# A Fourier layer and a gated feed-forward layer on one core: the end of batch 0's last inverse step moved into the first two token tiles, and the bias sum shared between GpSimd and TensorE

## The chip, the cores and the metric

One core of a Trainium2 chip. The metric is the device time of one execution in microseconds (us). Each kernel was timed in several executions. The profile is of one execution.

## The reference

```python
# attention part: b = 8 batches, 3008 positions, 256 channels
X = np.fft.rfft(x, axis=1)
Yr = Xr @ w_r - Xi @ w_i + b_r
Yi = Xr @ w_i + Xi @ w_r + b_i
# soft threshold of Yr and Yi at 0.01, then
y = np.fft.irfft(Y, n=3008, axis=1)
# feed-forward part on 24064 tokens, d_ff = 2048
h = y @ w_in
r = np.maximum(h, 0.0)
g = s * (r * r) + b
out = g @ w_out
```

The constant b contributes b times the column sums of w_out to each row of the output. The kernel computes that once, as `bias_bc`.

## The kernel before

The transform of 3008 = 94 x 32 points is done by matmuls. Batch 0 is transformed alone at the start (some 47 us). After that TensorE works through token tiles, and the transforms of the later batches are interleaved with the tiles in small units. Batch 0 ends with a transpose back (`turn`) and the last DFT (`last_dft`), for two halves ec of the 256 channels and for 32 values of n2. The first three token tiles read only n2 below 16.

```python
# end of first_batch(), ec = 1 (the second half of the channels e)
for k in range(4):
    turn(1, k)            # two PSUM banks: 4 transposes and a copy of 512 columns each
    some(1)               # a matmul of batch 1's first step (u)
    if k:
        last_dft(1, 8 * (k - 1))   # two banks: 4 DFTs and a copy of 384 columns each
last_dft(1, 24)
...
def evac(dst, src, cols, scale=None):    # a copy out of PSUM, to the less loaded engine
    ta, td = 0.17 + cols / 1200.0, 0.15 + cols / 960.0
    if load["act"] + ta <= load["dve"] + td:
        load["act"] += ta
        ...                               # ScalarE
    load["dve"] += td
    ...                                   # VectorE
...
def sum_w_out():          # GpSimd: all 16 row groups of w_out, in fp32
    for q in range(4, MC, 2):
        nc.gpsimd.tensor_tensor(out=acc, in0=acc, in1=w_out_t[:, q : q + 2], op=ALU.add)
    nc.gpsimd.tensor_tensor(out=w_sum, in0=acc[:, 0], in1=acc[:, 1], op=ALU.add)
def make_bias():          # one matmul with ones adds the 128 partitions
    nc.tensor.matmul(ps[:, 0:D], ones, w_sum, start=True, stop=True)
...
# in a token tile, for each pair of 128 columns of d_ff:
nc.scalar.activation(out=rt, in_=ps, func=AF.Relu)                   # ScalarE
nc.vector.tensor_tensor(out=gt, in0=rt, in1=rt, op=ALU.mult)         # the square, VectorE (or ScalarE, by load)
...
load.update(act=0.0, dve=0.0)    # between first_batch() and the tiles
```

The PSUM pool of the tiles (`psh`, two buffers of two banks) takes the place of the first batch's pool (`psm`, four banks). `psf` and `psa` have two banks each.

Of the kernel before, what the change touches and what calls it, by code (L numbers as in the profile page):

```python
# [9 lines left out]
F16 = mybir.dt.float16  # L10
F32 = mybir.dt.float32
ALU = mybir.AluOpType
AF = mybir.ActivationFunctionType

P = 128
N1 = 94
N2 = 32
# [79 lines left out]
def kernel(  # L97
# [13 lines left out]
    nc = tc.nc  # L111
    B, S, D = x.shape
# [4 lines left out]
    MC = DFF // P  # L117
    H = NPAIR // 2
    HW = N2 // 2
# [24 lines left out]
    cpool = ctx.enter_context(tc.tile_pool(name="consts", bufs=1))  # L144
# [20 lines left out]
    def evac(dst, src, cols, scale=None):  # L165
# [3 lines that stand above are left out]
            if scale is None:  # L169
                return None, nc.scalar.copy(out=dst, in_=src)  # L170
            return None, nc.scalar.mul(out=dst, in_=src, mul=scale)
        load["dve"] += td
        if scale is None:
            return nc.vector.tensor_copy(out=dst, in_=src), None
        return nc.vector.tensor_scalar_mul(out=dst, in0=src, scalar1=scale), None
# [3 lines left out]
    def mix_bank():  # L179
        return pools["m"].tile([P, 512], F32, name="psm", tag="psm")  # L180
# [3 lines left out]
    def any_bank():  # L184

        turn_of[0] += 1
        if "h" in pools:
            return (other_bank, one_bank)[turn_of[0] % 2]()
        return (mix_bank, one_bank, mix_bank, other_bank)[turn_of[0] % 4]()
# [4 lines left out]
    def one_bank():  # L194
        return fpool.tile([P, 512], F32, name="psf", tag="psf")

    def other_bank():
        return apool.tile([P, 512], F32, name="psa", tag="psa")
# [20 lines left out]
    ones = cpool.tile([P, P], F16, name="ones")  # L219
# [33 lines left out]
    eye_t = cpool.tile([P, P], F16, name="eye_t")  # L253
# [7 lines left out]
    bb_bc = cpool.tile([P, 1], F32, name="bb_bc")  # L261
# [22 lines left out]

    w_in_t = [cpool.tile([P, DFF], F16, name=f"w_in_{dc}") for dc in range(DC)]
    w_out_t = cpool.tile([P, MC, D], F16, name="w_out_t")
    bias_bc = cpool.tile([P, 2, D], F32, name="bias_bc")

    def emit_load_weights():
        for dc in range(DC):  # L290
            nc.gpsimd.dma_start(out=w_in_t[dc], in_=moe_w_in[dc * P : (dc + 1) * P, :])
        nc.gpsimd.dma_start(
            out=w_out_t, in_=moe_w_out.rearrange("(mc p) d -> p mc d", p=P)
        )


    neg_lam = cpool.tile([P, 1], F32, name="neg_lam")
# [35 lines left out]
            )  # L333
            nc.vector.tensor_copy(out=blocks(F_2[0])[r, :, 1, a], in_=F_c[r, :, 0])

    w_sum = cpool.tile([P, D], F16, name="w_sum")

    def sum_w_out():
        acc = opool.tile([P, 2, D], F32, name="acc", tag="ost")
        nc.gpsimd.tensor_tensor(  # L340
            out=acc, in0=w_out_t[:, 0:2], in1=w_out_t[:, 2:4], op=ALU.add
        )
        for q in range(4, MC, 2):
            nc.gpsimd.tensor_tensor(out=acc, in0=acc, in1=w_out_t[:, q : q + 2], op=ALU.add)
        nc.gpsimd.tensor_tensor(out=w_sum, in0=acc[:, 0], in1=acc[:, 1], op=ALU.add)

    def make_bias():
        ps = other_bank()
        nc.tensor.matmul(ps[:, 0:D], ones, w_sum, start=True, stop=True)
        for j in range(2):  # L350
            nc.scalar.activation(
                out=bias_bc[:, j], in_=ps[:, 0:D], func=AF.Copy, scale=bb_bc
            )

    us = {}
    vs = {}
# [6 lines left out]
    def first_batch():  # L363
# [3 lines left out]
        for g in range(N2 // 4):  # L367
            c, h = divmod(g, 2)
            for dc in range(DC):
                ps = one_bank() if dc else mix_bank()  # L370
                with tc.issue_after(last_pe.ins):
                    for j in range(4):
# [4 lines left out]
                            start=True, stop=True,  # L377
# [35 lines left out]
        vt = bigpool.tile([P, DC, N2, 96], F16, name="vt", tag="corr")  # L413
# [69 lines left out]
        for h in range(2):  # L483
            vs[(0, h)] = vspool.tile([96, HW, D], F16, name="vs", tag="vs")

        def turn(ec, k):
            for i in range(2):
                ps = any_bank() if ec else mix_bank()
                n = 8 * k + 4 * i
                for j in range(4):  # L490
                    nc.tensor.matmul(
                        ps[0:96, j * P : j * P + P], vt[:, ec, n + j, :], eye_t,
                        start=True, stop=True,
                    )
                h, n = divmod(n, HW)
                evac(
                    vs[(0, h)][:, n : n + 4, ec * P : (ec + 1) * P],
                    ps[0:96].rearrange("p (j e) -> p j e", e=P), 512,
                )

        yt = yts[0] = ypool.tile([P, DC, N2, 96], F16, name="yt", tag="yt")

        def last_dft(ec, n2):

            if ec or n2 >= 16:
                ps = [any_bank(), any_bank()]
            else:
                ps = [one_bank(), other_bank()]
            for j in range(8):
                h, k = divmod(n2 + j, HW)  # L510
                nc.tensor.matmul(
                    ps[j // 4][:, (j % 4) * 96 : (j % 4) * 96 + 96],
                    vs[(0, h)][:, k, ec * P : (ec + 1) * P], C_t,
                    start=True, stop=True,
                )
            for i in range(2):
                evac(
                    yt[:, ec, n2 + 4 * i : n2 + 4 * i + 4, :],
                    ps[i][:, 0:384].rearrange("p (j n) -> p j n", n=96), 384,
                )  # L520

        more = s1_units(1, True)

        def some(n):
            for _ in range(n):
                if more:
                    more.pop(0)()

        steps = [(ec, u) for ec in range(DC) for u in range(U)]
        for i in range(2 * U + 2):  # L530
            if i < 2 * U:
                mix(*steps[i])
            if 0 <= i - 1 < 2 * U:
                fwd_dft(*steps[i - 1])
            if 0 <= i - 2 < 2 * U:
                inv_dft(*steps[i - 2])
            k = i - U - 2
            if 0 <= k < 4:
                turn(0, k)
            for n in {1: (0,), 2: (8,), 4: (16, 24)}.get(k, ()):  # L540
                last_dft(0, n)
            if i >= 2 * U:
                some(3)
            if i == 9:

                gate = nc.gpsimd.tensor_copy(out=low[0:1, 0, 0:1], in_=vt[0:1, 1, 0, 0:1])
                with tc.issue_after(gate.ins):
                    make_w_g()
                    make_bounds()
                    sum_w_out()  # L550
        for k in range(4):
            turn(1, k)
            some(1)
            if k:
                last_dft(1, 8 * (k - 1))
        last_dft(1, 24)
        return more


    def s1_units(b, more_banks=False):  # L560
# [264 lines left out]
    def second_mms(ti):  # L825

        tl = tiles[ti]
        w = width(tl)
        size = sub_size(tl)
        nsub = -(-w // size)  # L830
        hold = {}

        def mm(sub, mc):

            alone = ti == len(tiles) - 1 and sub >= 2
            h = 0 if alone else sub % 2
            if h == 0 and mc == 0:
                hold["ps"] = other_bank().rearrange("p (h e) -> p h e", h=2)
            ps = hold["ps"]
            nc.tensor.matmul(  # L840
                ps[0:size, h, :], gts[(ti, mc // 2)][:, mc % 2, sub * size : (sub + 1) * size],
                w_out_t[:, mc, :],
                start=(mc == 0), stop=(mc == MC - 1),
            )
            if sub == nsub - 1 and mc % 2 == 1:
                gts.pop((ti, mc // 2))
            if mc == MC - 1 and (alone or h == 1 or sub == nsub - 1):
                k = h + 1
                ost = opool.tile([P, 2, D], F32, name="ost", tag="ost")
                nc.vector.scalar_tensor_tensor(  # L850
                    out=ost[0:size, 0:k], in0=ps[0:size, 0:k], scalar=s_bc[0:size],
                    in1=bias_bc[0:size, 0:k], op0=ALU.mult, op1=ALU.add,
                )
                load["dve"] += 0.12 + 0.27 * k
                for i in range(k):
                    store(tl, sub - k + 1 + i, ost[:, i, :])

        return [lambda s=s, m=m: mm(s, m) for s in range(nsub) for m in range(MC)]


    plan = {}

    def schedule(start, span, units):
        for i, u in enumerate(units):
            plan.setdefault(start + (i * span) // len(units), []).append(u)

    with tc.tile_pool(name="psm", bufs=4, space=bass.MemoryType.PSUM) as pool:
        pools["m"] = pool
        more = first_batch()
    pools["h"] = ctx.enter_context(  # L870
        tc.tile_pool(name="psh", bufs=2, space=bass.MemoryType.PSUM)
    )
# [6 lines left out]
        if tl[0] == "main" and tl[2] == 0 or tl[0] == "wide" and tl[2] == (0, 0):  # L879
            mark[tl[1]] = i * MC  # L880
    schedule(0, 10, more)
    plan.setdefault(15, []).append(make_bias)
    plan.setdefault(17, []).append(load_x_2)
    schedule(24, 42, s23_units(1))
    schedule(mark[1] - 12, 16, s4_units(1))
    for b in range(2, B):
# [51 lines left out]
```

## Time and profile before

| | us |
|---|---|
| time, median of the first 3 runs | 847.02 (846.86 to 847.43) |
| span of the profiled execution | 845.0 |
| first w_in matmul (first token tile) | 47.90 |
| GpSimd ends the sum of w_out | 50.00 |
| first matmul of batch 1's forward transform | 62.91 |

The page's first part gives each engine's busy time; the chain that ended last is followed back from the end, so an engine's share of it is time that counted. The timeline lists start, length, engine, line, operation and tiles, and in square brackets how long the engine had been idle and what ended that. Three lines of before's timeline are needed later, GpSimd's last add, VectorE's first four squares and the first forward matmul of batch 1 (columns as said):

```profile
49.28 0.72 POOL L345 TENSOR_TENSOR w_sum<-acc 128x256 f16<-128x256 f32 x1
...
50.15 4.67 DVE L783 TENSOR_TENSOR gt<-rt 128x1024 f16<-128x1024 f32 x4 [1.18 <-ACT rt L776]
...
62.91 0.61 PE L606 MATMUL psf<-F_t,us 128*128 128x128 f16 x8
```

GpSimd ends at 50.00, 0.15 us before the first square starts. Four squares take 4.67 us, 1.15 us from start to start.

### The profile page before, as it was taken

Reading aid. Unit: us, or ns where it says so; the run is one execution under the profiler, and the core shown is the slowest. Engines: PE = TensorE matmul, PEld = TensorE weight load, DVE = VectorE, ACT = ScalarE, POOL = GpSimd, SP = SyncE. Lnnn points to the kernel's source line nnn. Section 1 sums busy time; section 2 is a strip of 40 time slices with the busy share of each in tenths; the row PEclk is TensorE's granted clock in tenths of the full one; section 3 lists DMA queues with packets and bytes.
Section 4 is the critical chain, followed back from the end, with each engine's and each line's share of the span. In section 5 each row is a group of like instructions: output and inputs, shape, how many; then the busy total and the mean of one; then the engine's idle time right before and its main releaser. Section 6 shows DMA issues by size and latency. Waiting matters only on the chain.

```text
span 845.0 us, 17114 instructions
## 1 busy us (share of the span) xinstructions
PE 833.8 (99%) x6653; PEld 599.6 (71%) x6653; DVE 693.6 (82%) x1026; ACT 641.8 (76%) x864; POOL 45.0 (5%) x71
## 2 busy tenths in 40 slices
PE   8999999999999999999999999999999999999997
PEld 6857767777677766777677776777667777766765
DVE  5989987888888987888888888798978888776674
ACT  5988887778778877787777787778877878766673
POOL 5331000000000001000000000000000000000000
PEclk9999999999999999999999999999999999999999
DMA  8945567124752367324761248513354223411111
GB/s 202 180 143 122 121 173 203 57 77 101 203 154 56 101 169 190 92 68 107 189 175 49 81 103 205 160 42 91 113 144 125 64 74 95 112 33 38 38 44 50
DMA packets 105746, 96.06 MB, mean 114 GB/s; under 512 B 9542, under 2 KB 97482, under 8 KB 104322
## 3 DMA queue, kind: packets, MB, share of 16 engines
q1 hardware_dynamic: 99218, 80.55, 33.0%
q0 software_dynamic: 6448, 14.42, 10.6%
q8 instruction: 52, 0.85, 0.4%
q14 instruction: 28, 0.23, 0.1%
HBM read 53.52 MB, written 46.66 MB: 119 GB/s over the span
## 4 chain that ended last, share of the span: by engine, by line
PE 90%; ACT 3%; DMA 3%; DVE 2%; issue 1%; POOL 0%; SPq 0%; ACTq 0%; DVEq 0%; POOLq 0%
PE psa L840 37%; PE psh L769 36%; PE psf L635 4%; PE psf L570 2%; PE psf L621 2%; PE psf L606 2%; PE psf L665 2%; PE psf L718 2%; ACT rt L776 2%; PE psm L426 1%; DMA x<-in_x_dram 1%; DMA ud<-u 1%; DVE gt L783 1%; DMA us<-ud 1%; DMA F_c<-dft_fwd 0%
## 5 line engine op out<-in xcount | busy, mean ns | idle before, releaser
L776 ACT ACTIVATE rt<-psh 128x1024 f32<-128x1024 f32 (+2 forms) x384 | 386.7, 1008 | 119.6 <-PE psh L769 117.5
L783 DVE TENSOR_TENSOR gt<-rt 128x1024 f16<-128x1024 f32 (+2 forms) x322 | 385.7, 1202 | 95.4 <-ACT rt L776 94.5
L840 PE MATMUL psa<-w_out_t,gt 128*128 128x256 f16 (+1 forms) x3024 | 454.4, 272 | 0.1
L840 PEld LDWEIGHTS <-gt 128*128 128x128 f16 (+1 forms) x3024 | 300.9, 101 | 187.0 <-issue 1.4
L769 PE MATMUL psh<-yt,w_in 128*128 128x512 f16 (+1 forms) x1344 | 396.3, 378 | 0.2 <-ACT rt L776 0.2
L769 PEld LDWEIGHTS <-w_in 128*128 128x128 f16 x1536 | 142.8, 98 | 27.3 <-issue 1.8
L850 DVE SCALAR_TENSOR_TENSOR ost<-psa,s_bc,bias_bc 128x512 f32<-128x512 f32 (+2 forms) x97 | 71.1, 733 | 10.0 <-PE psa L840 8.2
L780 ACT ACTIVATE gt<-rt 128x1024 f16<-128x1024 f32 (+2 forms) x62 | 65.3, 1054 | 1.0
L640 DVE TENSOR_TENSOR ring<-psf,s 128x512 f16<-128x512 f32 x84 | 57.5, 685 | 3.8 <-PE psf L635 3.3
L170 ACT CAST v<-psf 128x512 f16<-128x512 f32 x78 | 45.3, 583 | 19.7 <-PE psf L665 19.7
L170 ACT CAST xf<-psf 128x512 f16<-128x512 f32 x82 | 47.9, 586 | 10.9 <-PE psf L606 10.9
L170 ACT CAST u<-psf 96x512 f16<-96x512 f32 x76 | 43.9, 580 | 12.4 <-PE psf L570 12.2
L769 PE MATMUL psh<-tail,w_in 128*128 128x512 f16 (+1 forms) x192 | 52.1, 353 | 0.0
L635 PE MATMUL psf<-W_g,xf 128*128 128x256 f16 x336 | 50.4, 273 | 0.0
L170 ACT CAST yt<-psf 128x480 f16<-128x480 f32 (+2 forms) x73 | 37.8, 525 | 11.6 <-PE psf L718 11.6
L213 POOL DMA_DIRECT2D x<-in_x_dram x36 | 18.7, 526 | 430.3 <-PE psf L570 429.2
L570 PE MATMUL psf<-x,A_t 94*96 94x512 f16 x103 | 39.3, 382 | 1.1 <-ACT yt L170 0.5
L646 DVE TENSOR_TENSOR ring<-ring,high 128x512 f16<-128x512 f16 x84 | 35.6, 423 | 2.3
L647 DVE TENSOR_TENSOR ring<-ring 128x512 f16<-128x512 f16 x84 | 35.5, 423 | 2.0
L645 DVE TENSOR_TENSOR ring<-ring,low 128x512 f16<-128x512 f16 x84 | 35.4, 421 | 1.6
L635 PEld LDWEIGHTS <-xf 128*128 128x128 f16 x336 | 32.9, 98 | 3.8
L718 PE MATMUL psf<-C_t,vs 96*128 96x96 f16 x448 | 33.2, 205 | 0.2 <-ACT yt L170 0.2
(97 smaller groups left out, 499.5 us busy)
## 6 DMA issues: line engine op xcount, KB each, us to landing
out_dram<-ost SPq DMA_DIRECT2D x152, 128.0 KB
ud<-u SPq DMA_DIRECT2D x28, 384.0 KB
us<-ud SPq DMA_DIRECT2D x28, 384.0 KB
vd<-v SPq DMA_DIRECT2D x42, 256.0 KB
vs<-vd SPq DMA_DIRECT2D x14, 768.0 KB
x<-in_x_dram POOLq DMA_DIRECT2D x28, 376.0 KB, 5.9
ring<-ring SPq DMA_DIRECT2D x280, 32.0 KB
out_dram<-ost SPq DMA_DIRECT2D x16, 120.0 KB
```

Source lines behind the costliest of these rows:

```text
L170: return None, nc.scalar.copy(out=dst, in_=src)
L570: nc.tensor.matmul(ps[0:96, :], A_t[0:N1, :], x16[(b, c)][0:N1, j * D : (j + 2) * D], start=True, stop=True,)
L635: nc.tensor.matmul(ps[:, r, :], xt[:, 2 - r, dc], W_g[:, dc, r], start=(dc == 0), stop=(dc == DC - 1),)
L640: nc.vector.tensor_tensor(out=t, in0=ps, in1=hold[i // 2][:, i % 2].unsqueeze(1).to_broadcast([P, 2, D]), op=ALU.add,)
L646: nc.vector.tensor_tensor(out=m, in0=m, in1=high, op=ALU.min)
L718: nc.tensor.matmul(ps[:, j * 96 : (j + 1) * 96], vs[(b, h)][:, k, ec * P : (ec + 1) * P], C_t, start=True, stop=True,)
L769: nc.tensor.matmul(o, w_in_t[dc][:, mc * P : (mc + 1) * P], r, start=(dc == 0), stop=(dc == DC - 1),)
L776: nc.scalar.activation(out=rt[:, :, 0:w], in_=ps[:, :, 0:w], func=AF.Relu)
L780: nc.scalar.activation(out=gt[:, :, 0:w], in_=rt[:, :, 0:w], func=AF.Square)
L783: nc.vector.tensor_tensor(out=gt[:, :, 0:w], in0=rt[:, :, 0:w], in1=rt[:, :, 0:w], op=ALU.mult)
L840: nc.tensor.matmul(ps[0:size, h, :], gts[(ti, mc // 2)][:, mc % 2, sub * size : (sub + 1) * size], w_out_t[:, mc, :], start=(mc == 0), sto ...
L850: nc.vector.scalar_tensor_tensor(out=ost[0:size, 0:k], in0=ps[0:size, 0:k], scalar=s_bc[0:size], in1=bias_bc[0:size, 0:k], op0=ALU.mult, o ...
```

## The change

Its intent: the first token tiles need only half of n2, so the other half of ec = 1 need not hold them up. Its transposes and last DFTs go into slots 10 to 24 of the tiles (a slot is one group of 128 columns of d_ff). The tiles then start earlier, and the bias must be ready earlier; so GpSimd adds 12 of the 16 row groups of w_out and TensorE accumulates the other four and the two halves of GpSimd's sum in PSUM.

```diff
-        nc.gpsimd.dma_start(
-            out=w_out_t, in_=moe_w_out.rearrange("(mc p) d -> p mc d", p=P)
-        )
+        for q in (slice(0, 12), slice(12, MC)):
+            nc.gpsimd.dma_start(out=w_out_t[:, q], in_=...[:, q])
 ...
-        for q in range(4, MC, 2):
+        for q in (4, 6, 8):
             nc.gpsimd.tensor_tensor(out=acc, in0=acc, in1=w_out_t[:, q : q + 2], op=ALU.add)
-        nc.gpsimd.tensor_tensor(out=w_sum, in0=acc[:, 0], in1=acc[:, 1], op=ALU.add)
+        nc.gpsimd.tensor_tensor(out=w_sum, in0=acc, in1=w_out_t[:, 10:12], op=ALU.add)
 ...
-        nc.tensor.matmul(ps[:, 0:D], ones, w_sum, start=True, stop=True)
+        parts = [w_out_t[:, q] for q in range(12, MC)] + [w_sum[:, 0], w_sum[:, 1]]
+        for i, part in enumerate(parts):
+            nc.tensor.matmul(ps[:, 0:D], ones, part, start=(i == 0), stop=(i == len(parts) - 1))
 ...  (turn and last_dft now do one bank of four n2 at a time)
-        for k in range(4):
-            turn(1, k)
-            ...
-        last_dft(1, 24)
-        return more
+        turn(1, 0); turn(1, 4); some(1); turn(1, 8); turn(1, 12); some(1)
+        last_dft(1, 0); last_dft(1, 4); some(2); last_dft(1, 8); last_dft(1, 12)
+        rest = [lambda n=n: turn(1, n) for n in range(HW, N2, 4)]
+        rest += [lambda n=n: last_dft(1, n) for n in range(HW, N2, 4)]
+        return rest, more
 ...
     schedule(0, 10, more)
-    plan.setdefault(15, []).append(make_bias)
-    plan.setdefault(17, []).append(load_x_2)
+    schedule(10, 6, rest[:4])
+    schedule(17, 10, rest[4:])
+    plan.setdefault(14, []).append(make_bias)
+    plan.setdefault(18, []).append(load_x_2)
```

`bias_bc` is also held once in place of twice, and the output's VectorE instruction reads it through a broadcast view.

More of the change, by code (lines that the diff above doesn't have):

```diff
@@ L286 @@
     w_out_t = cpool.tile([P, MC, D], F16, name="w_out_t")
-    bias_bc = cpool.tile([P, 2, D], F32, name="bias_bc")
+    bias_bc = cpool.tile([P, D], F32, name="bias_bc")
     def emit_load_weights():
@@ L291, in emit_load_weights @@
             nc.gpsimd.dma_start(out=w_in_t[dc], in_=moe_w_in[dc * P : (dc + 1) * P, :])
-        nc.gpsimd.dma_start(
-            out=w_out_t, in_=moe_w_out.rearrange("(mc p) d -> p mc d", p=P)
-        )
+        for q in (slice(0, 12), slice(12, MC)):
+            nc.gpsimd.dma_start(
+                out=w_out_t[:, q], in_=moe_w_out.rearrange("(mc p) d -> p mc d", p=P)[:, q]
+            )
     neg_lam = cpool.tile([P, 1], F32, name="neg_lam")
@@ L334, in place_f_2 @@
             nc.vector.tensor_copy(out=blocks(F_2[0])[r, :, 1, a], in_=F_c[r, :, 0])
-    w_sum = cpool.tile([P, D], F16, name="w_sum")
+    w_sum = cpool.tile([P, 2, D], F16, name="w_sum")
     def sum_w_out():
@@ L342, in sum_w_out @@
         )
-        for q in range(4, MC, 2):
+        for q in (4, 6, 8):
             nc.gpsimd.tensor_tensor(out=acc, in0=acc, in1=w_out_t[:, q : q + 2], op=ALU.add)
-        nc.gpsimd.tensor_tensor(out=w_sum, in0=acc[:, 0], in1=acc[:, 1], op=ALU.add)
+        nc.gpsimd.tensor_tensor(out=w_sum, in0=acc, in1=w_out_t[:, 10:12], op=ALU.add)
     def make_bias():
         ps = other_bank()
-        nc.tensor.matmul(ps[:, 0:D], ones, w_sum, start=True, stop=True)
-        for j in range(2):
-            nc.scalar.activation(
-                out=bias_bc[:, j], in_=ps[:, 0:D], func=AF.Copy, scale=bb_bc
+        parts = [w_out_t[:, q] for q in range(12, MC)] + [w_sum[:, 0], w_sum[:, 1]]
+        for i, part in enumerate(parts):
+            nc.tensor.matmul(
+                ps[:, 0:D], ones, part, start=(i == 0), stop=(i == len(parts) - 1)
             )
+        nc.scalar.activation(out=bias_bc, in_=ps[:, 0:D], func=AF.Copy, scale=bb_bc)
     us = {}
@@ L484, in first_batch, with turn, last_dft @@
             vs[(0, h)] = vspool.tile([96, HW, D], F16, name="vs", tag="vs")
-        def turn(ec, k):
-            for i in range(2):
-                ps = any_bank() if ec else mix_bank()
-                n = 8 * k + 4 * i
-                for j in range(4):
-                    nc.tensor.matmul(
-                        ps[0:96, j * P : j * P + P], vt[:, ec, n + j, :], eye_t,
-                        start=True, stop=True,
-                    )
-                h, n = divmod(n, HW)
-                evac(
-                    vs[(0, h)][:, n : n + 4, ec * P : (ec + 1) * P],
-                    ps[0:96].rearrange("p (j e) -> p j e", e=P), 512,
-                )
-        yt = yts[0] = ypool.tile([P, DC, N2, 96], F16, name="yt", tag="yt")
-        def last_dft(ec, n2):
-            if ec or n2 >= 16:
-                ps = [any_bank(), any_bank()]
-            else:
-                ps = [one_bank(), other_bank()]
-            for j in range(8):
-                h, k = divmod(n2 + j, HW)
+        def turn(ec, n):
+            ps = mix_bank() if ec == 0 else any_bank() if n < HW else one_bank()
+            for j in range(4):
+                nc.tensor.matmul(
+                    ps[0:96, j * P : j * P + P], vt[:, ec, n + j, :], eye_t,
+                    start=True, stop=True,
+                )
+            h, k = divmod(n, HW)
+            evac(
+                vs[(0, h)][:, k : k + 4, ec * P : (ec + 1) * P],
+                ps[0:96].rearrange("p (j e) -> p j e", e=P), 512,
+            )
+        yt = yts[0] = ypool.tile([P, DC, N2, 96], F16, name="yt", tag="yt")
+        def last_dft(ec, n):
+            if ec and n >= HW:
+                ps = one_bank()
+            elif ec or n >= HW:
+                ps = any_bank()
+            else:
+                ps = other_bank() if n % 8 else one_bank()
+            for j in range(4):
+                h, k = divmod(n + j, HW)
                 nc.tensor.matmul(
-                    ps[j // 4][:, (j % 4) * 96 : (j % 4) * 96 + 96],
+                    ps[:, j * 96 : j * 96 + 96],
                     vs[(0, h)][:, k, ec * P : (ec + 1) * P], C_t,
@@ L515, in last_dft @@
                 )
-            for i in range(2):
-                evac(
-                    yt[:, ec, n2 + 4 * i : n2 + 4 * i + 4, :],
-                    ps[i][:, 0:384].rearrange("p (j n) -> p j n", n=96), 384,
-                )
+            evac(
+                yt[:, ec, n : n + 4, :],
+                ps[:, 0:384].rearrange("p (j n) -> p j n", n=96), 384,
+            )
         more = s1_units(1, True)
@@ L538, in first_batch @@
             if 0 <= k < 4:
-                turn(0, k)
-            for n in {1: (0,), 2: (8,), 4: (16, 24)}.get(k, ()):
+                turn(0, 8 * k)
+                turn(0, 8 * k + 4)
+            for n in {1: (0, 4), 2: (8, 12), 4: (16, 20, 24, 28)}.get(k, ()):
                 last_dft(0, n)
@@ L550, in first_batch @@
                     sum_w_out()
-        for k in range(4):
-            turn(1, k)
-            some(1)
-            if k:
-                last_dft(1, 8 * (k - 1))
-        last_dft(1, 24)
-        return more
+        turn(1, 0)
+        turn(1, 4)
+        some(1)
+        turn(1, 8)
+        turn(1, 12)
+        some(1)
+        last_dft(1, 0)
+        last_dft(1, 4)
+        some(2)
+        last_dft(1, 8)
+        last_dft(1, 12)
+        rest = [lambda n=n: turn(1, n) for n in range(HW, N2, 4)]
+        rest += [lambda n=n: last_dft(1, n) for n in range(HW, N2, 4)]
+        return rest, more
     def s1_units(b, more_banks=False):
@@ L851, in mm @@
                     out=ost[0:size, 0:k], in0=ps[0:size, 0:k], scalar=s_bc[0:size],
-                    in1=bias_bc[0:size, 0:k], op0=ALU.mult, op1=ALU.add,
+                    in1=bias_bc[0:size].unsqueeze(1).to_broadcast([size, k, D]), op0=ALU.mult, op1=ALU.add,
                 )
@@ L868 @@
         pools["m"] = pool
-        more = first_batch()
+        rest, more = first_batch()
     pools["h"] = ctx.enter_context(
```

## The prediction

> **What bounds the kernel now.** I read the page first, the chain that ended last second, then the timeline of the changed stretch, 41 to 63 us. From the page, engines' busy time and the chain's shares:
>
> ```profile
> PE 833.8 (99%) x6653; PEld 599.6 (71%) x6653; DVE 693.6 (82%) x1026; ACT 641.8 (76%) x864; POOL 45.0 (5%) x71
> ...
> PE 90%; ACT 3%; DMA 3%; DVE 2%; issue 1%; POOL 0%; SPq 0%; ACTq 0%; DVEq 0%; POOLq 0%
> ```
>
> TensorE is busy nearly everywhere and holds 90% of the chain. GpSimd holds none: what is taken off it is not on the path. Where is TensorE not the bound? The chain of waits between 37 and 51 us:
>
> ```profile
> 40.56 0.61 DVE vt L174
> 41.17 0.04 issue
> 41.21 0.42 PE psa L491 x4
> 41.63 0.24 PE psm L491 x4
> 41.87 0.02 issue
> 41.89 1.07 ACT vs L170 x2
> 42.96 0.49 ACT u L170
> 43.45 0.38 ACT yt L170
> 43.83 0.49 ACT vs L170
> 44.31 0.49 ACT u L170
> 44.80 0.49 ACT vs L170
> 45.29 0.49 ACT u L170
> 45.77 0.39 ACT yt L170
> 46.16 0.04 issue
> ```
>
> Here the copies out of PSUM (0.49 us from start to start on ScalarE for 512 columns, 0.38 for 384) set the pace, not the matmuls. This is the end of batch 0's transform, which the change shortens. What ends it, from the timeline:
>
> ```profile
> 47.22 0.56 DVE L174 CAST yt<-psm 128x384 f16<-128x384 f32 x1 [0.61 <-PE psm L511]
> ...
> 47.90 1.89 PE L769 MATMUL psh<-yt,w_in 128*128 128x512 f16 x8
> ...
> 49.10 1.94 ACT L776 ACTIVATE rt<-psh 128x1024 f32<-128x1024 f32 x2 [0.42 <-DVE u L174]
> ```
>
> The token tiles' PSUM (psh) takes over the banks of psm, so the first tile starts at 47.90, right after the last copy out of psm ends (47.22 + 0.56 = 47.78). In the tiles the chain is a steady beat of TensorE, two w_in and four w_out matmuls:
>
> ```profile
> 816.17 0.43 PE psh L769 x2
> 816.60 0.44 PE psa L840 x4
> ```
>
> **What the Trainium skill says.** "TensorE: Matmul & The Clock Gate", section "Wait — 56ns, not 53.3ns?": warm matmuls start N / 2.4 GHz + 2.5 ns apart, so 215.8 ns for 512 columns, 109.2 for 256, 55.8 for 128, 42.5 for 96. The trace agrees: two of 512 and four of 256 take 0.43 + 0.44 = 0.87 us (2 x 215.8 + 4 x 109.2 = 868 ns). "Perfetto Trace Analysis", section "Tensor Engine Instruction (MATMUL, LD_WEIGHTS)": a matmul's end in the profile is an estimate from its size; agreed, since a 512-column row says 378 ns. So "busy 2.00 of 2.00" between 52 and 60 us is no proof of a full TensorE, and I count work by the start-to-start times instead. "GPSIMD Engine Reference", section "3.1 Elementwise — side-by-side cycle accounting": about 2.6 cycles per element for a two-input operation, so by its 1.2 GHz 1.11 us for 512 elements, an estimate; the row of w_out's sum says 1.15 us.
>
> **How much TensorE idles in the stretch, before.** Between the ninth-last u matmul of batch 1 (start 42.14) and the first matmul of batch 1's forward transform (62.91) the program order, which I had for both kernels, has 48 w_in + 9 u matmuls of 512 columns, 32 w_out and 1 bias of 256, 16 transposes of 128 and 32 last DFTs of 96: 57 x 0.2158 + 33 x 0.1092 + 16 x 0.0558 + 32 x 0.0425 = 18.16 us of work in 20.77 us: 2.61 us idle. Of these 1.78 lie before 47.90 (3.98 us of work in 5.76) and 0.83 after it (14.18 in 15.01). Beyond 62.9 the profile shows hardly a wait of TensorE, up to the last tile. So 2.61 us is all that the move can win, 0.3% of the span.
>
> **The change part by part.**
>
> (1) *The move.* 16 transposes and 16 last DFTs with their eight copies (four of 512 columns, four of 384) leave the stretch before the tiles. By rows, the copies are 4 x 0.49 + 4 x 0.38 = 3.5 us of ScalarE time, shared by two engines about 1.8 us, or 2.4 by the VectorE's longer 0.68 and 0.54. I stepped the new order through with these durations. Both kernels run the same instructions to 43.5. Then ScalarE: yt 43.33, u 43.70, yt 44.18, u 44.6, u 45.1, u 45.6. VectorE: yt 43.48, u 43.94, yt 44.54 (the last copy out of psm, ends 45.08), u 45.0, u 45.6. The last u matmul ahead of the first tile waits for a psf bank, and goes at about 45.2. First tile: **45.4 in place of 47.9, 2.5 us earlier**. TensorE's idle time before the tiles falls from 1.78 to 45.4 - 42.14 - 2.41 of work = 0.87: a gain of 0.91 us.
>
> (2) *The same work comes back inside the tiles*: 16 x (0.0558 + 0.0425) = 1.57 us of TensorE, and eight copies, six on ScalarE and two on VectorE by the new order. There ScalarE sets the beat of the first tile: relu (rt) 0.97 us from start to start for each pair of w_in groups, whose TensorE time is 4 x 0.2158 = 0.86. I stepped this too: each w_in group waits for the relu two before it. The first transposes and the bias fill these gaps; TensorE idles in pieces of 0.05 to 0.2 us, 0.8 us in all, until the w_out matmuls flow at about 54.9. From there it never waits: the relus stay ahead. So the tiles keep their 0.8 us idle, and the moved work costs its TensorE time, which was paid before as well.
>
> (3) *The bias.* One 256-column matmul becomes six: **+5 x 0.1092 = 0.55 us on TensorE**, which is the bound. GpSimd loses four of its adds, 4 x 1.22 us (spacing in the trace) = 4.9 us, but nobody waits for it: w_sum ends at 50.0 and its reader starts at 51.95. Even with the tiles 2.5 us earlier, the stepped order reaches the bias at 52.0 to 53.9, after 50.0. One ScalarE bias copy (0.48 us) goes as well.
>
> (4) *The store's operand* becomes a broadcast view: no change of its 0.73 us, and VectorE is not the bound later.
>
> Sum: front -0.91, tiles about -0.03, bias +0.55: **-0.4 us**. Check: 45.4 + 16.30 of work (14.18 + 1.57 + 0.55) + 0.8 idle = 62.5 against 62.91. From there TensorE's order is the same but for two swapped rows, so the gain stays as it is: 847.0 - 0.4 = **846.6 us**.
>
> **Rivals.**
>
> *ScalarE becomes the bound in the first two tiles.* Twelve relus, one u, two vs, one bias copy, four yt: 12 x 0.98 + 0.49 + 2 x 0.55 + 0.48 + 4 x 0.45 = 15.6 us from 46.5, to 62.1, as long as TensorE needs. For it: ScalarE and VectorE show 2.00 of 2.00 there now. Against: the last yt copies come when the relus are already ahead. If it holds, the moved copies cost about 1 us and the kernel is at 847 to 848.
>
> *All idle time closes.* If the transposes fill the first tile's gaps wholly, the gain is 2.61 - 0.55 = 2.1 us: 844.9. Against: the relu's beat leaves gaps whatever fills them, and a slot's filler is shorter or longer than its gap.
>
> *A wait for w_sum is removed.* The intent may be that GpSimd would come too late after the move. If w_sum were late in the old form by 1 us, the split would pay for its 0.55. The trace speaks against it (50.0 against 52.0).
>
> *A DMA takes over.* Batch 1's second-stage input (us) is loaded from about 54.6 and needed at 62.8; its last u copy now ends some 2.5 us earlier, its need 0.4 earlier. No new wait.
>
> **Range and chances.** Every route lies within 845 to 848, a quarter of a per cent; the runs before spread 0.57 us. I centre on 846.5, a little to the side of more gaps filled, and allow 845.2 to 847.6. Nothing here can move 17 us: faster 0.01, same 0.98, slower 0.01.
>
> **What the changed profile would show.** The first w_in matmul at 45.4 (between 45.0 and 46.0), relu at 46.5. The first matmul of batch 1's forward transform at 62.5: later than 62.9 means that ScalarE bound the tiles (then waits of TensorE for relu or for copies in the psf bank, after 55 us), 61 means that the gaps closed. No wait of the bias matmuls for GpSimd, whose last add ends near 46. Past 63 us the same beat of 0.87 us. I am wrong if the copies placed between relus delay these by more than the gaps hold, or if the different split of later copies between ScalarE and VectorE opens new waits further on.

## The result, and the profile after

The changed kernel took **847.38 us** (median of 6 runs, 847.10 to 847.72), the kernel before 847.16 us in the same rounds (846.86 to 848.13). The ratio is 1.0001, with a 95% interval of 0.9988 to 1.0014. The time is the same. It lies inside the predicted range (845.2 to 847.6), near its upper end and 0.9 us above its centre of 846.5.

The page of the changed kernel, the same two lines as shown of before in the prediction:

```profile
PE 835.2 (99%) x6658; PEld 600.6 (71%) x6658; DVE 693.8 (82%) x1027; ACT 641.3 (76%) x862; POOL 42.9 (5%) x69
...
PE 91%; DMA 3%; ACT 3%; DVE 2%; issue 1%; POOL 0%; DVEq 0%; ACTq 0%; POOLq 0%
```

Little has moved on this level: five matmuls more, and GpSimd 2.1 us less busy. The chain of waits in the changed stretch (start, length, what was on the chain):

```profile
41.81 0.42 PE psa L494 x4
42.23 0.24 PE psm L494 x4
42.47 0.02 issue
42.49 1.07 ACT vs L170 x2
43.56 0.49 ACT u L170
44.05 0.38 ACT yt L170
44.42 0.49 ACT u L170
44.91 0.39 ACT yt L170
45.30 0.04 issue
```

The row of copies on ScalarE is three links shorter than before. The timeline shows what it leads to:

```profile
45.14 0.55 DVE L174 CAST yt<-psm 128x384 f16<-128x384 f32 x1
...
45.54 1.15 POOL L348 TENSOR_TENSOR w_sum<-acc,w_out_t 128x512 f16<-128x512 f32 x1
...
46.05 1.89 PE L782 MATMUL psh<-yt,w_in 128*128 128x512 f16 x8
...
48.30 4.67 DVE L796 TENSOR_TENSOR gt<-rt 128x1024 f16<-128x1024 f32 x4 [1.43 <-ACT rt L789]
...
62.97 0.39 PE L619 MATMUL psf<-F_t,us 128*128 128x128 f16 x4
```

The first token tile starts at 46.05 in place of 47.90. But batch 1's first forward matmul comes at 62.97, against 62.91. Part of that is the run: the whole stretch from the transposes on (41.81 against 41.21, in code that is the same in both kernels) lies 0.60 us later in this execution. To take that out I count from the first transposes of ec = 1, the first row of the chain above. The table has the starts of the same four matmuls in every profiled execution: the first w_in matmul, batch 1's first forward matmul (near 63 us), the 144th w_in matmul (near 120 us), and the last matmul of the kernel. It is read from the traces, instruction by instruction in each one's order.

| kernel | first transposes at | first w_in | first forward | 144th w_in | last | between forward and 144th |
|---|---|---|---|---|---|---|
| before | 41.21 | +6.69 | +21.70 | +78.76 | +799.30 | 57.06 |
| before, again (e1) | 41.15 | +6.69 | +22.00 | +79.05 | +799.60 | 57.05 |
| changed | 41.81 | +4.24 | +21.16 | +79.32 | +799.63 | 58.16 |
| changed, again (e2) | 41.75 | +4.24 | +21.16 | +79.36 | +799.36 | 58.20 |
| move only (e3) | 41.60 | +4.24 | +22.56 | +80.73 | +800.65 | 58.17 |
| copies uncounted (e4) | 41.17 | +4.24 | +21.16 | +78.19 | +798.94 | 57.03 |
| one bias matmul, wrong (e5) | 41.18 | +4.24 | +20.78 | +78.98 | +798.90 | 58.20 |
| four idle adds more (e6) | 43.17 | +4.24 | +22.75 | +80.96 | +800.87 | 58.21 |
| before, copies counted (e7) | 41.40 | +6.69 | +21.98 | +80.12 | +800.05 | 58.14 |
| uncounted, 14 of 16 (e8) | 41.60 | +4.24 | +21.45 | +78.48 | +800.52 | 57.03 |
| w_out first (e9) | 41.22 | +4.24 | +20.78 | +77.81 | +798.35 | 57.03 |
| split only (e10) | 41.21 | +6.69 | +22.21 | +79.27 | +799.87 | 57.06 |
| copies uncounted, again (e11) | 41.78 | +4.24 | +21.20 | +78.22 | +799.11 | 57.02 |

So the changed kernel is 0.54 us ahead at 63 us (21.70 - 21.16), 0.56 us behind at 120 us, and at the end level within the scatter of two profiles of one kernel (799.63 and 799.36 against 799.30 and 799.60). Two questions follow: what loses 1.1 us between 63 and 120 us, and what the two halves of the change are each worth.

### The profile page after: what moved, and what is told of

Same layout as the page of the kernel before. It is cut to its first block, busy times and chain, and to the rows that moved or that the text cites. A ratio compares the mean times of both kernels' runs of the same rounds, so it can differ in the third digit from the quotient of the medians. Undisturbed runs are those within 1.5% of the kernel's fastest.

```text
span 845.9 us, 17109 instructions
## 1 busy us (share of the span) xinstructions
PE 835.2 (99%) x6658; PEld 600.6 (71%) x6658; DVE 693.8 (82%) x1027; ACT 641.3 (76%) x862; POOL 42.9 (5%) x69
## 4 chain that ended last, share of the span: by engine, by line
PE 91%; DMA 3%; ACT 3%; DVE 2%; issue 1%; POOL 0%; DVEq 0%; ACTq 0%; POOLq 0%
PE psh L782 37%; PE psa L853 37%; PE psf L648 4%; PE psf L583 3%; PE psf L634 2%; PE psf L619 2%; PE psf L678 2%; PE psf L731 2%; ACT rt L789 1%; DMA ud<-u 1%; PE psm L430 1%; DMA x<-in_x_dram 1%; DMA F_c<-dft_fwd 1%; PE psf L460 0%; DMA ring<-ring 0%
## 5 line engine op out<-in xcount | busy, mean ns | idle before, releaser
L793 ACT ACTIVATE gt<-rt 128x1024 f16<-128x1024 f32 (+2 forms) x65 | 68.2, 1050 | 1.0
```

The costliest lines, as they stand in the source:

```text
L793: nc.scalar.activation(out=gt[:, :, 0:w], in_=rt[:, :, 0:w], func=AF.Square)
```

## The experiments

My theory after the two traces had three parts. (A1) The bias matmuls cost their TensorE time, and GpSimd was never waited for. (A2) The loss beyond 63 us comes from the running loads: the eight copies that now fall after the loads' reset are counted in them, and so every later copy and square is given out differently. (A3) The 0.6 us at the start is the run's. Rivals stand with each run. e1 to e4 ran together on one chip, e5 to e8 on a second and e9 to e11 on a third; each group was timed against its own runs of the kernel before.

### e1 and e2: both kernels once more

No edit: the same two kernels.

> The kernel before, unchanged, timed against itself and profiled a second time: it measures what is only the run. Theory A (the 0.6 us by which the changed kernel's transform starts later, +0.60 us from 16 us on in a stretch where both kernels have the same instructions, is the run's input loads): here too the first w_in matmul lies within 47.3 to 48.5 and everything moves by one shift of up to 0.6 us, ratio 0.9995 to 1.0005. Rival B (the stalls beyond 63 us change from run to run as well): then the last matmul's time less the first transposes' time differs from the first profile of before by 0.3 us or more; under A it differs by less than 0.15 us.

> The changed kernel, unchanged, on the same chip as the others. Theory A: the distance from the first transposes to the first w_in matmul is again 4.24 us (6.69 in the kernel before), and the net loss beyond 63 us comes back (+0.9 us between 63 and 120 us against before, +0.3 us at the end from the transposes on). Rival B (run noise): the stalls beyond 63 us fall elsewhere, net between -0.5 and +0.5 us. Ratio to before 0.999 to 1.001 under both.

Measured: before again 847.40 us against 847.28, ratio 1.0001 (0.9989 to 1.0014); changed again 846.91 us, ratio 0.9995 (0.9983 to 1.0008). The losses of the changed kernel came back in the same places: 58.20 us between forward and 144th, against 58.16, so they belong to the kernel and not to the run. The +0.3 us expected at the end did not come back (799.36 - 799.30 = 0.06). (A3) is not settled by these two, since each kernel kept its start (41.15 and 41.21, 41.75 and 41.81); what supports it is e4 and e11, one kernel on two chips, whose first transposes come at 41.17 and 41.78, and e2 and e4, on one chip and with the same code up to there (41.75 and 41.17). Not expected: the repeat of before is 0.30 us later at the end, the mark set for the rival. But it is so at the first forward matmul already and gains nothing after it. Its timeline shows why:

```profile
49.84 0.73 POOL L345 TENSOR_TENSOR w_sum<-acc 128x256 f16<-128x256 f32 x1
...
50.09 1.56 DVE L783 TENSOR_TENSOR gt<-rt 128x1024 f16<-128x1024 f32 x1 [1.18 <-ACT rt L776]
```

Here w_out landed a little later, GpSimd's last add ended at 50.57, and the square that started beside it took 1.56 us where the others take 1.21.

### e3: the move without the split

```diff
-        for q in (4, 6, 8):
+        for q in range(4, MC, 2):
 ...
-        parts = [w_out_t[:, q] for q in range(12, MC)] + [w_sum[:, 0], w_sum[:, 1]]
+        parts = [w_sum]          # GpSimd adds all row groups, one load of w_out
```

> The move without the split of the bias: GpSimd adds all of w_out's rows and TensorE does one 256-column bias matmul, all else as in the changed kernel. Theory A (the bias matmuls cost their TensorE time, GpSimd was never waited for): w_sum ends near 50 us, before its reader near 52, no wait for GpSimd, and batch 1's first forward matmul comes 0.55 us earlier relative to the transposes than in the changed kernel; time 0.3 to 0.6 us lower than the changed kernel. Rival (the split is what lets the tiles start earlier): the bias matmul waits for GpSimd, TensorE stands for up to 1 us there, and the kernel is as slow as the changed one or slower by 0.5. Second rival (the bias matmuls lay in gaps that the relus leave): within 0.15 us of the changed kernel at that point.

Measured: 848.84 us against 847.28, ratio 1.0013 (1.0000 to 1.0027), and 1.40 us behind the changed kernel at the first forward matmul (22.56 - 21.16). The opposite of what I expected, though the bias matmul shows no wait for GpSimd either (it starts at 52.42, right behind the transposes before it, and 0.10 us after the last add's end). The timeline (a row with x2 or x4 is merged, the others are single instructions):

```profile
47.40 3.25 POOL L347 TENSOR_TENSOR acc<-acc,w_out_t 128x512 f32<-128x512 f32 x2
...
48.63 2.02 POOL L347 TENSOR_TENSOR acc<-acc,w_out_t 128x512 f32<-128x512 f32 x1
...
48.09 6.44 DVE L796 TENSOR_TENSOR gt<-rt 128x1024 f16<-128x1024 f32 x4 [1.43 <-ACT rt L789]
...
49.55 2.18 DVE L796 TENSOR_TENSOR gt<-rt 128x1024 f16<-128x1024 f32 x1
...
55.19 0.38 PE L494 MATMUL psf<-eye_t,vt 128*96 128x128 f16 x4 [1.27 <-DVE vs L174]
```

Where GpSimd's adds (normally 1.15) and VectorE's squares (1.21) meet, one takes 2.02 and the other 2.18: each waits for the other to end. The square at 49.55 ends about when it would if it had begun at 50.65, the end of the add. Four squares take 6.44 us in place of 4.67. VectorE then comes late to a copy out of a psf bank, and TensorE stands for 1.27 us. The Trainium skill has this: "SBUF — State Buffer", section "Who interferes with whom", says that a VectorE instruction with two inputs in SBUF contends with a GpSimd instruction that reads SBUF, by an exclusive lock. This trace agrees to 0.13 us (51.73 against 50.65 + 1.21). VectorE's copies out of PSUM are not touched: 0.68 us beside the adds and after them. The 1.40 us are net of what the five matmuls fewer save. Against e9 below, which has the same order of instructions on TensorE, ScalarE and VectorE from the first transposes to the first forward matmul and differs in when GpSimd adds, the overlap costs 1.78 us (22.56 - 20.78).

### e6: the suspected cost added by itself

```diff
         nc.gpsimd.tensor_tensor(out=w_sum, in0=acc, in1=w_out_t[:, 10:12], op=ALU.add)
+        for _ in range(4):       # read by nobody
+            nc.gpsimd.tensor_tensor(out=acc, in0=acc, in1=w_out_t[:, 10:12], op=ALU.add)
```

> The changed kernel with four more GpSimd adds after w_sum, read by nobody, so that they run beside VectorE's first squares. Theory A (a GpSimd add and a VectorE square of two operands in SBUF slow each other, and that is what cost the move-only run 1.2 us): the squares beside them take 1.6 us from start to start in place of 1.17, the adds 1.5 in place of 1.2, TensorE waits about 1 us for a copy by VectorE out of a psf bank near 54 us, and the first forward matmul comes 0.8 to 1.4 us later than in the changed kernel. Rival (in the move-only run something else, as the reader's wait for w_sum, held TensorE): squares stay at 1.17, no shift over 0.1 us.

Measured: 849.55 us against 847.23, ratio 1.0027 (1.0015 to 1.0040). The first forward matmul comes 1.59 us later than in the changed kernel (22.75 - 21.16), a little more than I had said. The timeline:

```profile
47.00 5.72 POOL L350 TENSOR_TENSOR acc<-acc,w_out_t 128x512 f32<-128x512 f32 x4
...
49.66 6.42 DVE L798 TENSOR_TENSOR gt<-rt 128x1024 f16<-128x1024 f32 x4 [1.43 <-ACT rt L791]
...
53.90 2.16 ACT L791 ACTIVATE rt<-psh 128x1024 f32<-128x1024 f32 x2 [0.58 <-DVE gt L798]
...
54.97 1.02 PE L784 MATMUL psh<-yt,w_in 128*128 128x512 f16 x4 [0.61 <-ACT rt L791]
```

Adds that nobody reads, on an engine that is 5% busy, cost the kernel 1.6 us. The path is plain: slow squares hold the three rt buffers, the relu waits for one (0.58), and TensorE for the relu (0.61); at 56.73 TensorE stands another 0.73 us for a VectorE copy out of a psf bank, as expected. The squares took up to 2.17 us, where I had said 1.6. The adds are the only thing changed here, so the overlap by itself costs the 1.6 us; e9 shows the other side, the whole sum without the overlap and without the cost. (This profile also began 1.36 us later than that of the changed kernel, ahead of any of this code, with longer waits for the first loads of x; it isn't counted in the 1.59. By the clock the kernel is 2.3 us above before.)

### e5: the bias matmuls by themselves

```diff
-        parts = [w_out_t[:, q] for q in range(12, MC)] + [w_sum[:, 0], w_sum[:, 1]]
+        parts = [w_sum[:, 0]]    # wrong result on purpose
```

> Wrong result on purpose: the changed kernel whose bias takes one 256-column matmul over a quarter of what it should add, GpSimd's work unchanged (it ends near 46.7, before the first square). Measures the five further bias matmuls by themselves. Theory A (they lie on TensorE, which is the bound): batch 1's first forward matmul comes 0.55 us earlier relative to the first transposes than in the changed kernel (21.16 us after them there), and the end with it. Rival (they fill gaps that the relus of the first tile leave anyway): 0.0 to 0.25 us earlier. The move-only run could not tell, as its GpSimd adds ran into the squares.

Measured: a wrong result (relative error 0.49); 846.57 us against 847.23, ratio 0.9991 (0.9978 to 1.0003). The first forward matmul comes 0.38 us earlier (21.16 - 20.78). That lies between my theory (0.55) and the rival (at most 0.25): about a third of the five matmuls' time fell into gaps that the relus left.

### e10: the split without the move

```diff
 # kernel before
-        for q in range(4, MC, 2):
+        for q in (4, 6, 8):
 ...
-        nc.tensor.matmul(ps[:, 0:D], ones, w_sum, start=True, stop=True)
+        parts = [w_out_t[:, q] for q in range(12, MC)] + [w_sum[:, 0], w_sum[:, 1]]
+        for i, part in enumerate(parts):
+            nc.tensor.matmul(ps[:, 0:D], ones, part, start=(i == 0), stop=(i == len(parts) - 1))
 # and w_out in two loads
```

> The kernel before with the other half of the change alone: GpSimd adds 12 of 16 row groups, TensorE does six bias matmuls. Theory A: first w_in matmul 6.69 us after the transposes as before; GpSimd ends near 46.5, no square is slow; the five further matmuls cost TensorE 0.3 to 0.55 us, so the first forward matmul comes 22.0 to 22.3 us after the transposes (21.70 and 22.00 in the two profiles of before, the latter with one slow square). Rival (the split gains by itself): 21.4 or less.

Measured: 847.74 us against 847.27, ratio 1.0003 (0.9991 to 1.0016). The first forward matmul comes at +22.21, 0.51 us after that of before (21.70), 0.21 us after its repeat with one slow square. By itself the split only costs. So each half alone is a loss at 63 us (+0.51 split, +0.86 move) and both together are a gain (-0.54): the split clears the squares for the move.

### e4 and e11: the moved copies not counted in the loads

```diff
-    def evac(dst, src, cols, scale=None):
+    def evac(dst, src, cols, scale=None, on=None):
+        if on == "act":
+            return None, nc.scalar.copy(out=dst, in_=src)
+        if on == "dve":
+            return nc.vector.tensor_copy(out=dst, in_=src), None
 ...
-        rest = [lambda n=n: turn(1, n) for n in range(HW, N2, 4)]
-        rest += [lambda n=n: last_dft(1, n) for n in range(HW, N2, 4)]
+        rest = [lambda n=n: turn(1, n, "dve" if n % 8 else "act") for n in range(HW, N2, 4)]
+        rest += [lambda n=n: last_dft(1, n, "act") for n in range(HW, N2, 4)]
```

The copies go to the same engines as in the changed kernel. From the first forward matmul on, ScalarE and VectorE then have the sequence of the kernel before, but for one moved copy that is still to come; so the traces show, and also that e7 has the changed kernel's.

> The changed kernel with one difference: the eight copies that moved into the tiles go to the same engines as now, but are not counted in the running loads by which later copies and squares are given to ScalarE or VectorE. From the first forward matmul on, the order on ScalarE and VectorE is then that of the kernel before. Theory A (the gain of about 0.5 us at 63 us is lost again because later copies are split differently and open new short waits): the shift against before stays near its value at 63 us, -0.5 us from the transposes on, to the end; time 0.6 to 0.9 us below the changed kernel. Rival (the losses come from the order of TensorE and the banks near 63 us, whoever copies): the loss of 0.4 us between 63 and 71 us stays, and the kernel is within 0.3 us of the changed one.

> The run with uncounted copies once more, beside the two above. Theory A: 4.24 us to the first w_in matmul and 21.16 us to the first forward matmul, no loss between 63 and 120 us against before, time 846.6. Rival (its lead of 0.7 us was chance): 847.2 or more, or jumps between 63 and 120 us.

Measured: e4 846.60 us against 847.28, ratio 0.9993 (0.9980 to 1.0005); e11 847.18 us against 847.27, ratio 0.9998 (0.9985 to 1.0010). By the clock e4 is 0.3 us below the changed kernel of the same rounds (846.91), less than the 0.6 to 0.9 expected and about what its rival allowed, and e11, where 846.6 was expected, is level with before. So the clock does not decide. The start of a run (41.17 and 41.78 here) and two load waits (0.21 us near 543 us in e4, 0.34 near 147 in e11) scatter by as much. At the expected place the trace is clear: 57.03 and 57.02 us between forward and 144th, as before (57.06), where the changed kernel takes 58.16. At the 144th w_in matmul both are 0.5 us ahead of before (78.19 and 78.22 against 78.76); at the last, after those load waits, by 0.36 and 0.19 (799.30 - 798.94 and - 799.11).

### e7: the counting without the copies

```diff
 # kernel before
     schedule(0, 10, more)
+    schedule(10, 6, [lambda: count(512)] * 4)     # count() adds to load["act"] or
+    schedule(17, 10, [lambda: count(384)] * 4)    # load["dve"] as evac does, and emits nothing
```

> The kernel before with one difference: at the places in the token tiles where the change puts the eight copies, their cost is added to the running loads, without any copy. From the first forward matmul on its order on ScalarE and VectorE is that of the changed kernel. Theory A (the later split of copies alone loses 0.8 us): same times as before up to 62.9 us, then a loss of 0.6 to 0.9 us by 120 us in the same places (71, 84, 107 us), ratio about 1.0008. Rival (the losses belong to the changed arrival of data): no shift over 0.2 us at any place.

Measured: 847.65 us against 847.23, ratio 1.0003 (0.9991 to 1.0016), within noise by the clock. By the trace 58.14 us between forward and 144th: 1.08 us lost in the kernel before by numbers alone, no instruction added, where I expected 0.6 to 0.9. At the end 0.45 to 0.75 us of loss are left against the two profiles of before. (The first forward matmul is 0.28 us later than in the first profile of before, with one slow square, as in e1.) Through all thirteen profiles the stretch takes 57.0 or 58.2 us, according to the loads alone. Followed at each w_in matmul, the delay against before comes in steps; in the changed kernel the largest are +0.28 us near 71 us, +0.34 near 84 and +0.40 near 107, and -0.23 near 114. Of the places, the one near 107 us, in the timelines of before and of the changed kernel:

```profile
106.40 0.58 ACT L170 CAST u<-psf 96x512 f16<-96x512 f32 x1
...
106.72 1.22 DVE L783 TENSOR_TENSOR gt<-rt 128x1024 f16<-128x1024 f32 x1
107.07 0.38 PE L665 MATMUL psf<-ring,T_t 128*128 128x256 f16 x2
```

```profile
107.41 1.06 ACT L793 ACTIVATE gt<-rt 128x1024 f16<-128x1024 f32 x1
...
108.37 0.56 ACT L170 CAST u<-psf 96x512 f16<-96x512 f32 x1
...
108.67 0.38 PE L678 MATMUL psf<-ring,T_t 128*128 128x256 f16 x2 [0.24 <-DVE ring L653]
```

Before, the square of this pair is VectorE's and ScalarE copies u out of its psf bank at once. In the changed kernel ScalarE has the square first, the copy comes behind it, and with two psf banks, of which VectorE holds the other, the inverse transform's matmul waits: before, it took the bank that u's copy had set free at 106.98; now it takes VectorE's, free at 108.62, while u's copy ends at 108.93. That this is how the other steps arise too is not shown. The greedy rule balances sums of time; it doesn't know that a copy frees a bank and a square doesn't.

### e8: more of the sum back to GpSimd

```diff
 # e4, and
-        for q in (slice(0, 12), slice(12, MC)):
+        for q in (slice(0, 14), slice(14, MC)):
 ...
-        for q in (4, 6, 8):
+        for q in (4, 6, 8, 10):
 ...
-        parts = [w_out_t[:, q] for q in range(12, MC)] + ...
+        parts = [w_out_t[:, q] for q in range(14, MC)] + ...
```

> The changed kernel with the moved copies not counted in the loads, and GpSimd adding 14 of the 16 row groups of w_out in place of 12, which leaves TensorE four bias matmuls in place of six. Theory A: 0.22 us less TensorE work than the run with uncounted copies, GpSimd's last add ends near 48.0, just before the first square near 48.3, so no slow square: 0.8 us earlier than before from the first transposes on, time about 846.4. Rival (the last add reaches into the first square, or w_out's larger first load lands later): a slower first square and no gain over the uncounted run.

Measured: 846.55 us against 847.23, ratio 0.9992 (0.9978 to 1.0005), 0.68 us below before just as e4 is below its own, and no gain over e4 in the trace: +21.45 against +21.16. In this run w_out landed late, the last add ended at 48.73 after the first square's start at 48.09, and that square cost 0.5 us more. Two matmuls fewer didn't pay for it. The rival held in this execution; but it is the slowest of the five (848.34, the others 846.41 to 846.82, 1.2 us of that from waits for loads of us near 147 and 543 us), and whether the last add meets the square in the others is not shown.

### e9: w_out loaded first

Since only the end of GpSimd's work matters, and GpSimd stood 4.3 us for w_out, the sum can be started earlier in place of being shortened.

```diff
 # e4, with GpSimd's whole sum and one bias matmul as before, and
-        for dc in range(DC):
-            nc.gpsimd.dma_start(out=w_in_t[dc], ...)
         nc.gpsimd.dma_start(out=w_out_t, ...)
+        for dc in range(DC):
+            nc.gpsimd.dma_start(out=w_in_t[dc], ...)
```

> The move, with copies not counted in the loads, GpSimd adding all of w_out again and one bias matmul, but w_out loaded ahead of w_in so that GpSimd can start some 4 us earlier (it stood 4.3 us for w_out). Theory A (what the split buys is that GpSimd's adds end before VectorE's first square at about 48 us): the adds end near 46.5, the squares keep 1.15 us, and the first forward matmul comes 20.8 us after the first transposes, as in the run with one bias matmul (20.78) and before the uncounted run (21.16); time about 0.4 us below the uncounted run. Rival (w_out lands last whatever its place, or w_in then comes too late for the first tile): adds still end near 52 and squares of 1.6 us, 22.5 us; or a first w_in matmul later than 4.24 us after the transposes.

Measured: 846.34 us against 847.27, ratio 0.9986 (0.9972 to 1.0000), the lowest of all. The timeline:

```profile
36.92 7.31 POOL L350 TENSOR_TENSOR acc<-acc,w_out_t 128x512 f32<-128x512 f32 x6
44.31 0.72 POOL L351 TENSOR_TENSOR w_sum<-acc 128x256 f16<-128x256 f32 x1
...
47.71 4.67 DVE L799 TENSOR_TENSOR gt<-rt 128x1024 f16<-128x1024 f32 x4 [1.43 <-ACT rt L792]
```

GpSimd ends at 45.03, 2.7 us clear of the squares. The first forward matmul comes at +20.78, as in e5, and the lead of 0.92 us over before is kept to the end (798.35 against 799.30 and 799.60). It is a tenth of a per cent, and by the trace it leaves 1.7 us of the 2.61 us of idle TensorE that the prediction counted up to 63 us.

## Why the prediction was right or wrong

The time was in the range and the class was right, but neither says much: the range held a gain of 1.8 us as well as a loss of 0.6, and no route led to 2%. The 0.4 us forecast did not come (847.38 against 847.16); that the time stayed inside is the sum of a gain, a loss that the prediction did not count, and a part of it given back. Its steps:

- **The front** was right. Said: the first tile 2.5 us earlier. Measured: 2.45 (6.69 - 4.24). The time in the profile, 46.05 in place of 45.4, is 0.60 us of a later start of the run and 0.05 of error, and so just outside the 45.0 to 46.0 given. One reading was wrong: the tile does not start because the last copy out of psm ends. In both kernels it follows the last u matmul, 0.22 us after its start (47.68 and 47.90, 45.83 and 46.05), behind a wait of 0.28 or 0.30 us for a psf bank; the last copy out of psm ended 0.36 us before it in the changed kernel. The stepped order had this u matmul in it, so the sum did not suffer.
- **The tiles absorb the moved work** was right. The sum said 0.4 us ahead at the first forward matmul; measured 0.54. TensorE was not kept waiting by ScalarE after 55 us up to there, so the rival "ScalarE becomes the bound" fell; the gaps did not all close either: 16.92 us from the first w_in to the first forward matmul for 16.30 of work, 0.62 idle where 0.8 was said. The "2.00 of 2.00" quoted for ScalarE holds only to 56 us (1.80 and 1.78 in the two slices after it), and TensorE has 1.96 in the first slice.
- **The bias at 0.55 us** was mis-sized: 0.38 us in the changed kernel (e5), 0.51 in the kernel before (e10). With 0.38 the prediction's own sum gives the 0.54 ahead to 0.02. GpSimd's saving was mis-sized too, without effect: eight adds became five, not four fewer, and the sum takes 6.1 us in place of 9.3.
- **"nobody waits for it"**, said of GpSimd's adds, was the step that failed in its reason. Nobody waits by semaphore, but an add and a square exclude each other. With the tiles 2.5 us earlier the old sum would have run until 52.3 beside the squares and cost 1.40 us more than the split (e3; 1.78 by the overlap alone). I had looked for a late reader of w_sum and not for a neighbour on the port. In the sum the error stayed hidden, since both halves of the change were there.
- **"so the gain stays as it is"** failed, and it is why the time did not fall. The order on TensorE was the same but for some rows at 63 to 66 us and at 108 us, and I didn't follow the orders on ScalarE and VectorE further than the first tiles. 0.54 us ahead at 63 us became 0.56 us behind at 120 us (58.16 - 57.06 = 1.10 lost), through the loads (e4 keeps the gain, e7 has the loss alone). The prediction names this as what would make it wrong ("the different split of later copies"), without weight.
- What is given back later is the loads' too. Followed at each w_in matmul against before, the changed kernel (both profiles), e3, e5, e6 and e7 all gain 0.2 us near 147 us, 0.16 near 323 and 0.26 near 730, 0.6 in all; no run whose loads are those of before does. e7 has it with no instruction changed. So the other split of copies costs 1.1 us and returns 0.6; the net of 0.5 is as much as the change had won. The rest are waits for loads of us near 147 and 543 us, which differ between two profiles of one kernel (0.39 and 0.08 us near 543 in the changed kernel); what sets these was not tested.

## What to carry to other kernels

Read an engine's off-path work for what shares a port with it, not only for who waits for its result: the place of a few us of GpSimd adds was worth 1.6 to 1.8 us, and the cheapest cure was to start them earlier, by the order of two loads. When work moves across the point where a load balancer counts, check the order of every engine to the end of the program; here a balancer that weighs time but not what a copy sets free took back what the move had won. Where gains are of a tenth of a per cent, compare the starts of the same instructions, counted from a common one, since the clock's scatter is as large as the gain.

## What the Trainium skill lacked or had wrong

- "SBUF — State Buffer", section "Who interferes with whom", was right and was decisive; I found nothing there on how the lock looks in a profile. Here it lies inside the rows: an add of 2.02 us in place of 1.15, a square of 2.18 in place of 1.21. No idle time and no wait names it; the waits show only its consequence, TensorE 1.27 us for a VectorE copy.
- "Perfetto Trace Analysis", section "GPSIMD Engine Instruction", tells to treat a GpSimd row's length as unreliable. For these adds the row was 0.07 us short of the spacing: 1.15 us for each row and 1.22 from start to start (7.31 us for six); only rows that met a square were longer.
- "GPSIMD Engine Reference", section "3.1 Elementwise — side-by-side cycle accounting": an estimate of 1.11 us for 512 elements by its 2.6 cycles; 1.15 by row and 1.22 by spacing measured, so the estimate is up to a tenth low.
- "TensorE: Matmul & The Clock Gate", section "Wait — 56ns, not 53.3ns?": right for the steady beat (0.87 us). As a price of an added matmul it was too high here: five of 256 columns, 0.55 us by it, cost 0.38 where other waits left gaps and 0.51 where they left few.
